# The first weight load split over two hardware DMA queues, in a one-core gated decode block

## The chip, the core and the metric

The kernel runs on 1 core of one Trainium2 chip. The metric is device time in microseconds, from the start to the end of one execution on that core. The kernel before took 376.38 us (median of 3 runs, 376.34 to 377.0).

A core has a matrix engine (TensorE, PE in the profile), VectorE (DVE), ScalarE (ACT), GpSimd (POOL) and SyncE (SP). Data comes from the device's memory by DMA: an engine's sequencer issues a transfer, and the transfer's packets are carried by the 16 DMA engines that the profile counts. A transfer belongs to the queue of the engine that issued it. The profile of before shows two queues of kind "hardware_dynamic": q1, on which everything that SP issues goes, and q10, on which ScalarE's one transfer goes.

## What is computed

One token for each of B = 2 sequences, width D = 448. With xn the layer norm of x, the output is x + s * g, where s is grouped-query attention of xn over a cache (16 query heads, 8 key/value heads, 4096 positions, head width 256) and g is the SiLU of a bilinear feed-forward of xn:

```
def _A_ref(x, k_cache, v_cache, wq, wo):
    q = (lambda x, *d: x.transpose(*d))((x @ wq).reshape(B, Sq, Hq, Dh), 0, 2, 1, 3)
    ...
    scores = jnp.einsum("bhqd,bhkd->bhqk", q, k) * (Dh ** -0.5)
    p = _softmax(scores, axis=-1)
    o = jnp.einsum("bhqk,bhkd->bhqd", p, v)
    return (lambda x, *d: x.transpose(*d))(o, 0, 2, 1, 3).reshape(B, Sq, Hq * Dh) @ wo

def _B_ref(x, w_gate, w_up, w_down):
    g = jnp.einsum("bsd,df->bsf", x, w_gate)
    u = jnp.einsum("bsd,df->bsf", x, w_up)
    h = g * u
    return jnp.einsum("bsf,fd->bsd", h, w_down)

x = A_x
xn = _layernorm(x, axis=-1)
s = _A_ref(xn, A_k_cache, A_v_cache, A_wq, A_wo)
g = _silu(_B_ref(xn, B_w_gate, B_w_up, B_w_down))
return x + s * g
```

All data are float32. Keys and values alone are 134 MB; with the weights the profile counts 158.5 MB read.

## The kernel before

The whole job is a stream of loads with a little work on each. There are 16 pairs of a key/value head and a sequence, i = 0 to 15. `ring` has two buffers of 64 KB per partition (8 MiB each): one takes `first` (the keys of pair 0), and then each takes a `vk` load, the values of pair i beside the keys of pair i + 1. `slot` is a single buffer that holds one weight at a time: first wq0 (the half of the query weights for the first heads), later w_gate with w_up (`wgu`), w_down with the other half of wq (`wdq`), and most of wo.

`plan` (line 82) writes the list of loads, and `issue(n)` (line 62) issues the next n of them from SP, in order. A load whose buffer is still in use waits at SP's queue, together with everything behind it. The list starts with wq0, `first`, and the first vk load; `issue(3)` at line 94 sends these three. wgu waits until TensorE has finished with wq0 (the end of `query(0)`), and the next vk load until the scores of pair 0 have been computed from `first`.

wq0 comes as one transfer of 128 partitions x 26,624 bytes (line 75). Its last rows are stored apart: `wqx` (line 79) brings 16 partitions x 16,384 bytes into columns of the same slot that lie behind wq0.

x itself is tiny (2 x 448). Line 102 loads it into `x2`, a view of the tile `e0` that `early()` makes at line 100, from ScalarE's queue. GpSimd makes the identity matrix `ident` at line 104. Then comes a chain on VectorE: mean, centred x, sum of squares (lines 114 to 118), the power on GpSimd (line 120), the normed rows (123, 124), four transposes on TensorE (127) that need `ident`, and the copy to `xnT` (129). A like branch gives `xeT` (139) for the rows in wqx. With these and wq0, `query(0)` (line 317) multiplies: in `rows`, 12 matmuls at line 173, then those of lines 179 and 182 with wqx. VectorE turns the result into `qT` (195), and `scores(0)` (line 321) starts on `first`.

In the main loop (line 324), step i multiplies the probabilities with the values of pair i (line 277), computes the scores of pair i + 1 (line 245), issues the next load, scales the output (331) and runs the softmax (246 to 270). Feed-forward, second query half and the projection are fitted in at steps 0, 2, 4 and 8. After the loop the last pairs, the projection from wo2's pieces (line 313), the gate and x are put together (380, 381) and written at line 382.

Of the kernel before, what the change touches and what calls it, by code (L numbers as in the profile page):

```python
# [29 lines left out]
SIDE = 16  # L30
EXTRA = 8
# [8 lines left out]
def gated_decode_block(ctx: ExitStack, tc: tile.TileContext, x, first, vk, last0, last1, wq0, wqx, wdq, wo, wgu, out):  # L40
    nc = tc.nc
# [17 lines left out]
    loaded = {}  # L59
    todo = []  # L60

    def issue(n=1):
        for names, src, cuts in todo[:n]:
            weight = names[0].startswith("w")
            if weight:
                t = slot.tile([128, PART], F32, name="slot", align_bytes=512)
            else:
                t = ring.tile([128, 2 * ROW], F32, name="ring", align_bytes=512)
            width = ROW if not weight else src.shape[1] // len(names)
            for i, name in enumerate(names):  # L70
                loaded[name] = t[:, i * width:(i + 1) * width]
            if names == ["wd", "wq1"]:
                loaded["wd"], loaded["wq1"] = t[:, :14 * D], t[:, 14 * D:]
            for lo, hi in zip(cuts, cuts[1:]):
                nc.sync.dma_start(t[:, lo:hi], src[:, lo:hi])  # L75
            if names == ["wq0"]:
                at = src.shape[1]
                loaded["wqx"] = t[:, at:at + EXTRA * 512]
                nc.sync.dma_start(loaded["wqx"][:SIDE], wqx[:, :4])
        del todo[:n]  # L80

    def plan(names, src, cuts=None):
        todo.append((names.split(), src, cuts or [0, src.shape[1]]))
# [7 lines left out]
            plan(*weights[i])  # L91
    plan(f"k{LAST + 1} v{LAST}", last0, [0, ROW, 2 * ROW])
    plan(f"v{LAST + 1} wo2", last1, [0, 4096, 7168, *(ROW + i * D // 2 for i in (0, 6, 12, 14, 15, 16))])
    issue(3)


    def early():
        return [work.tile([128, 2, 512], F32, name=n, bufs=1)[:B] for n in ("p", "pT")]

    e0, e1 = early()  # L100
    x2 = e0[:, 0, :D]
    nc.scalar.dma_start(x2, x)
    ident = const.tile([128, 128], F32)
    make_identity(nc, ident)
    one = const.tile([1, 1], F32)
# [30 lines left out]
    for j in range(NK):  # L136
        at = 384 + j * SIDE
# [65 lines left out]
    def lift(ps):  # L203
        t = work.tile([128, D], F32, name="h")
        nc.scalar.copy(t, ps[:, :D])
        return t
# [113 lines left out]
    oT2 = const.tile([128, 1, 2, REP, W], F32)  # L320
    ss = scores(0)
    issue(2)
    p = over(softmax(*ss))
    for i in range(LAST):
        g, b = divmod(i, B)
        o = bank("o", 1)
        values(i, p[0], o)
        ss = scores(i + 1)

        issue(1 + (i + 1 in weights))  # L330
        nc.scalar.activation(ob[:, b * 4 + g if g < 4 else b * 3 + g - 4], o, AF.Copy, scale=p[1])  # L331
        if i == LAST - 1:
            cb = combine(ob, 6)
        p = softmax(*ss)
        if i < LAST - 1:
            p = over(p)
        if i == 7:
            cb = combine(ob, 8)
            for n in range(B):
                turn(oT0, cb[:, n * 256:(n + 1) * 256], 0, n, 4)  # L340
            ob = work.tile([128, 8, 512], F32, name="ob", bufs=1)
        if i in (0, 2, 4, 8):
            if i == 0:
                ffn_in()
            if i == 2:
                ffn_out()
            if i == 4:
                query(1)
            if i == 8:
                project(oT0, 0, 0, EARLY)  # L350
# [6 lines left out]
    t = lift(wide)  # L357
# [76 lines left out]
```

## Time and profile before

| | before |
|---|---|
| runs | 376.34, 376.38, 377.0 us |
| the profiled execution's own time | 376.44 us |
| its span in the trace | 374.7 us |
| DMA packets | 4357, 158.79 MB |
| mean rate over the span | 424 GB/s |
| mean granted TensorE clock | 0.752 |

The span is shorter than the execution's time because the trace begins with the first instruction and ends with the last. The times in the lines below are microseconds from the start of the span. In a line of the timeline the columns are start, length, engine, line, operation, output<-input and count, and in brackets the engine's idle time before it and what ended that. "SPq" and "ACTq" are the sequencers that issue transfers. In a line of the windows stand the stretch, its length, the busy time of TensorE, its weight loads, VectorE, ScalarE and GpSimd, each with the number of instructions, then the granted clock, the DMA share (1.00 is all 16 engines busy) and GB/s. In a queue row stand packets, MB and the share of the time of 16 engines.

The page's list of issues gives, for the transfers of the start, their sizes and the time from issue to landing: wq0 3328.0 KB in 10.7 us, `first` 4096.0 KB in 21.4 us, wqx 256.0 KB and x 3.5 KB without a landing time.

### The profile page before, as it was taken

The numbers are of one execution on the slowest core, as the hardware profiler recorded it, in microseconds if no ns is written. First come the engines' busy times: TensorE is split into PE (matmuls) and PEld (weight loads), VectorE is DVE, ScalarE is ACT, GpSimd is POOL, SyncE is SP. The second block draws the span as 40 slices with busy tenths as digits, with TensorE's granted clock in tenths as the row PEclk, the third lists the DMA queues.
The fourth block names the chain that finished last, engine by engine and source line by source line (L and its number), as shares of the span: only waits on it lengthen the run. The fifth ranks groups of instructions, "written<-read, shape, count | busy, mean of one in ns | idle before, by whom it ended". The sixth has DMA issues, their size and how long they took to land.

```text
span 374.7 us, 3272 instructions
## 1 busy us (share of the span) xinstructions
PE 209.0 (56%) x1472; PEld 63.0 (17%) x1472; DVE 63.2 (17%) x113; ACT 36.3 (10%) x56; POOL 1.2 (0%) x7
## 2 busy tenths in 40 slices
PE   1792468174736092869174666641718191909795
PEld 0110112021211020212021112210202020202232
DVE  4003021103030003030303030300211203020431
ACT  1001010001012002010101010100010101010120
POOL 1000000000000000000000000000000000000000
PEclk9968586657686567789758687865968776877899
DMA  8999899999999999999999999999999999999994
GB/s 322 438 500 434 374 439 448 441 443 435 425 429 448 441 441 393 429 448 436 427 448 434 436 422 409 444 448 434 441 428 429 441 441 406 450 409 434 415 418 181
DMA packets 4357, 158.79 MB, mean 424 GB/s; under 512 B 614, under 2 KB 1000, under 8 KB 1384
## 3 DMA queue, kind: packets, MB, share of 16 engines
q1 hardware_dynamic: 4340, 158.59, 98.2%
q8 instruction: 11, 0.18, 0.2%
q10 hardware_dynamic: 4, 0.00, 0.0%
q14 instruction: 2, 0.02, 0.0%
HBM read 158.54 MB, written 0.06 MB: 423 GB/s over the span
## 4 chain that ended last, share of the span: by engine, by line
DMA 76%; PE 22%; issue 0%; SPq 0%; DVE 0%
DMA ring<-vk 67%; PE o L277 11%; PE s L245 8%; DMA ring<-last 6%; DMA slot<-wq 3%; PE t L179 1%; PE t L173 1%; PE t L182 1%; SPq L75 0%; PE acc L313 0%; DVE qT L195 0%; DVE h L380 0%; DVE h L381 0%
## 5 line engine op out<-in xcount | busy, mean ns | idle before, releaser
L277 PE MATMUL o<-ring,pT 128*32 128x512 f32 x480 | 83.1, 855 | 91.5 <-DMA ring<-vk 91.5
L245 PE MATMUL s<-ring,qT 128*32 128x512 f32 x512 | 61.8, 624 | 2.4 <-ACT p L260 1.5
L246 DVE TENSOR_REDUCE m<-s 128x1 f32<-128x1024 f32 x16 | 19.6, 1225 | 222.1 <-PE s L245 222.1
L277 PEld LDWEIGHTS o<-ring,pT 128*32 128x32 f32 x480 | 21.2, 149 | 143.6 <-issue 142.0
L331 ACT ACTIVATE ob<-o,su 128x512 f32<-128x512 f32 x14 | 9.6, 688 | 190.7 <-PE o L277 190.7
L260 ACT ACTIVATE p<-s,m 128x1024 f32<-128x1024 f32 x16 | 17.8, 1114 | 97.5 <-DVE m L257 97.5
L245 PEld LDWEIGHTS s<-ring,qT 128*32 128x32 f32 x512 | 18.0, 115 | 44.6 <-issue 40.4
L263 DVE STREAM_TRANSPOSE pT<-p 128x1024 f32<-128x1024 f32 x15 | 18.7, 1245 | 21.2 <-ACT p L260 21.2
L269 PE MATMUL sm<-su,add_head 128*128 128x1 f32 x32 | 7.6, 305 | 22.9 <-ACT p L260 22.9
L251 PE MATMUL sm<-ident,m 128*1 128x128 f32 x16 | 4.3, 270 | 18.9 <-DVE m L246 18.8
L253 DVE TENSOR_REDUCE mx<-sm 1x128 f32<-1x512 f32 x16 | 10.8, 678 | 6.3 <-PE sm L251 6.3
L173 PE MATMUL t<-slot,xnT 128*32 128x512 f32 x48 | 8.8, 887 | 3.4 <-DMA slot<-wq 3.4
L269 PEld LDWEIGHTS sm<-su,add_head 128*128 128x128 f32 x32 | 6.2, 242 | 25.4 <-ACT p L260 24.1
L256 PE MATMUL sm<-one,mx 1*128 1x1 f32 x16 | 3.5, 218 | 12.3 <-DVE mx L253 12.3
L304 PE MATMUL wide<-slot,oT 128*32 128x448 f32 x48 | 7.2, 759 | 0.0
L173 PE MATMUL s<-slot,xnT 128*32 128x448 f32 x48 | 7.2, 748 | 0.1
L227 PE MATMUL t<-slot,hT 128*32 128x448 f32 x28 | 5.6, 911 | 2.4 <-DMA slot<-wdq 2.4
L251 PEld LDWEIGHTS sm<-ident,m 128*1 128x1 f32 x16 | 1.3, 79 | 33.0 <-DVE m L246 32.3
L286 PE MATMUL cb<-ob,add_blocks 128*32 128x64 f32 (+2 forms) x64 | 5.6, 475 | 0.8 <-ACT ob L372 0.8
L179 PE MATMUL t<-slot,oT 16*32 16x512 f32 x16 | 5.7, 703 | 0.0
L195 DVE STREAM_TRANSPOSE qT<-t 128x256 f32<-128x256 f32 x4 | 1.6, 428 | 19.8 <-PE t L179 15.2
L256 PEld LDWEIGHTS sm<-one,mx 1*128 1x128 f32 x16 | 2.1, 133 | 15.4 <-DVE mx L253 15.4
(71 smaller groups left out, 54.1 us busy)
## 6 DMA issues: line engine op xcount, KB each, us to landing
ring<-last SPq DMA_DIRECT2D x2, 4096.0 KB, 24.8
slot<-wdq SPq DMA_DIRECT2D x1, 6720.0 KB
slot<-wgu SPq DMA_DIRECT2D x1, 6272.0 KB, 34.3
slot<-wo SPq DMA_DIRECT2D x1, 5376.0 KB, 40.9
ring<-first SPq DMA_DIRECT2D x1, 4096.0 KB, 21.4
slot<-wq SPq DMA_DIRECT2D x1, 3328.0 KB, 10.7
ring<-last SPq DMA_DIRECT2D x1, 2048.0 KB, 14.7
ring<-last SPq DMA_DIRECT2D x1, 1536.0 KB
```

What stands on the lines that cost most here:

```text
L173: nc.tensor.matmul(ps[W * c:W * (c + 1), :n], xnT[:, k, :], block(NT * k + c), start=k == 0, stop=False)
L179: nc.tensor.matmul(ps[W * c:W * (c + 1), :n], xeT[:, j, :], extra[:SIDE, at:at + n], start=False, stop=j == NK - 1)
L227: nc.tensor.matmul(ps[W * t:W * (t + 1), :D], hT[:, i], loaded["wd"][:, i * D:(i + 1) * D], start=i < NT, stop=i >= 14 - NT)
L245: nc.tensor.matmul(s[W * c:W * (c + 1), h, :], q[:, d], k[:, h, d, c, :], start=d == 0, stop=d == 1)
L246: nc.vector.tensor_reduce(m[:, 0:1], s, axis=AX.XY, op=OP.max)
L253: nc.vector.tensor_reduce(mx, sm[:1, None, :128].rearrange("p o (c j) -> p o j c", c=NT).to_broadcast([1, NT, W, NT]), axis=AX.X, op=OP.max)
L260: nc.scalar.activation(p, s, AF.Exp, bias=m[:, 1:2], scale=1.0 / 16, accum_out=su[:, 0:1])
L263: nc.vector.transpose(pT.rearrange("p h n -> p (h n)"), p.rearrange("p h n -> p (h n)"))
L269: nc.tensor.matmul(sm[:, 130:131], add_head.rearrange("p a r j -> p (a r j)"), su[:, 0:1], start=True, stop=True)
L277: nc.tensor.matmul(o[W * t:W * (t + 1), :], pT[:, h, at:at + 2 * W:2], loaded[f"v{i}"][:, e * 512:(e + 1) * 512], start=e < NT, stop=e >= ...
L304: nc.tensor.matmul(wide[W * t:W * (t + 1), :D], heads(oT, i, first), loaded["wo"][:, i * D:(i + 1) * D], start=i < NT, stop=i >= LATE - NT)
L331: nc.scalar.activation(ob[:, b * 4 + g if g < 4 else b * 3 + g - 4], o, AF.Copy, scale=p[1])
```

## The change

wq0 is issued in two halves: partitions 64 to 127 from ScalarE's queue and partitions 0 to 63 from SP's. Between them and wqx, x is loaded from GpSimd's queue. Since `x2` must exist by then, `issue(3)` is moved behind `early()`. On ScalarE the half of wq0 stands where x's load was, as its first instruction; on GpSimd x's load stands ahead of the three instructions that make `ident`; on SP the order stays wq0 (now half), wqx, `first`, vk and so on. All later loads are as before, line numbers move by three to nine, and the order of the work on TensorE and VectorE is the same.

```diff
@@ -71,12 +71,17 @@
             if names == ["wd", "wq1"]:
                 loaded["wd"], loaded["wq1"] = t[:, :14 * D], t[:, 14 * D:]
+            if names == ["wq0"]:
+
+                at = src.shape[1]
+                nc.scalar.dma_start(t[64:, :at], src[64:])
+                nc.sync.dma_start(t[:64, :at], src[:64])
+                nc.gpsimd.dma_start(x2, x)
+                loaded["wqx"] = t[:, at:at + EXTRA * 512]
+                nc.sync.dma_start(loaded["wqx"][:SIDE], wqx[:, :4])
+                continue
             for lo, hi in zip(cuts, cuts[1:]):
                 nc.sync.dma_start(t[:, lo:hi], src[:, lo:hi])
-            if names == ["wq0"]:
-                at = src.shape[1]
-                loaded["wqx"] = t[:, at:at + EXTRA * 512]
-                nc.sync.dma_start(loaded["wqx"][:SIDE], wqx[:, :4])
         del todo[:n]
@@ -91,15 +96,13 @@
     plan(f"v{LAST + 1} wo2", last1, [0, 4096, 7168, *(ROW + i * D // 2 for i in (0, 6, 12, 14, 15, 16))])
-    issue(3)
-
 
     def early():
         return [work.tile([128, 2, 512], F32, name=n, bufs=1)[:B] for n in ("p", "pT")]
 
     e0, e1 = early()
     x2 = e0[:, 0, :D]
-    nc.scalar.dma_start(x2, x)
+    issue(3)
     ident = const.tile([128, 128], F32)
     make_identity(nc, ident)
```

## The prediction

> **What bounds the kernel now.** I began with the page: the engines' shares, the DMA row of the forty slices and the queue rows.
>
> ```profile
> span 374.7 us, 3272 instructions
> PE 209.0 (56%) x1472; PEld 63.0 (17%) x1472; DVE 63.2 (17%) x113; ACT 36.3 (10%) x56; POOL 1.2 (0%) x7
> DMA  8999899999999999999999999999999999999994
> ...
> q1 hardware_dynamic: 4340, 158.59, 98.2%
> q8 instruction: 11, 0.18, 0.2%
> q10 hardware_dynamic: 4, 0.00, 0.0%
> ```
>
> No compute engine is busy for more than 56% of the span, while the packets of one queue, q1, fill 98.2% of the time of all 16 DMA engines. q10 carries four packets of almost no bytes: that is x, the only load that ScalarE issues. Next I asked whether the DMA engines ever run dry in between, with the windows (the last two columns are the DMA share and GB/s).
>
> ```profile
> 50.00:100.00 50.00, 27.52 (x184) 7.99 (x180) 7.99 (x12) 3.84 (x7) 0.00 (x0) 0.69 1.01 435
> ...
> 200.00:250.00 50.00, 29.19 (x188) 9.19 (x188) 10.74 (x17) 4.99 (x8) 0.00 (x0) 0.76 1.00 433
> ...
> 300.00:340.00 40.00, 21.84 (x148) 6.73 (x144) 6.72 (x10) 3.79 (x6) 0.00 (x0) 0.71 0.99 426
> ```
>
> They don't: 426 to 435 GB/s with a share of about 1 from 50 to 340 us. The chain of waits, in order of time, begins and goes on like this:
>
> ```profile
> 0.74 10.72 DMA slot<-wq
> ...
> 24.16 5.73 PE s L245 x32
> 29.89 0.02 issue
> 29.91 47.01 DMA ring<-vk
> 76.92 0.14 issue
> 77.06 6.53 PE o L277 x32
> 83.59 3.47 PE s L245 x32
> 87.06 0.02 issue
> 87.08 44.35 DMA ring<-vk
> ```
>
> It names some 10 us of TensorE between two loads. Read beside the windows this isn't time lost: while TensorE works on one ring buffer (77.06 to 87.06), the load of the other is running at 435 GB/s. The real bound is one stream of bytes: 158.59 MB at 433 GB/s are 366.3 us of the 374.7. What delays or advances the whole stream at its start comes out at the end one for one, and what delays only the compute early on costs nothing.
>
> So the start of the stream matters:
>
> ```profile
> 0.00:1.50 1.50, 0.00 (x0) 0.00 (x0) 0.09 (x2) 0.19 (x1) 0.70 (x6) 1.00 0.00 0
> 1.50:1.75 0.25, 0.00 (x0) 0.00 (x0) 0.00 (x0) 0.25 (x1) 0.00 (x0) 1.00 0.13 7
> 1.75:2.00 0.25, 0.00 (x0) 0.00 (x0) 0.00 (x0) 0.25 (x1) 0.00 (x0) 1.00 4.09 958
> 2.00:4.00 2.00, 0.00 (x0) 0.00 (x0) 1.29 (x4) 0.59 (x1) 0.00 (x0) 1.00 0.74 280
> 4.00:6.00 2.00, 0.14 (x2) 0.14 (x2) 1.27 (x5) 0.00 (x0) 0.55 (x1) 1.00 0.99 426
> ```
>
> A packet is booked where it starts, which is why one window shows 958; 2 to 4 us then shows only 280, and from 4 us on it is 426. The first rows of wq0 thus start at about 1.75 us, 1.0 us after the issue at 0.74, and come in unevenly.
>
> **The change part by part.** The issues and the chain of x, from the timeline:
>
> ```profile
> 0.74 0.53 ACTq L102 DMA_DIRECT2D p<-x  x1
> 0.74 0.39 SPq L75 DMA_DIRECT2D slot<-wq  x1
> 1.02 0.29 POOL masks.py:199 TENSOR_SCALAR_AFFINE_SELECT ident<-ident 128x128 f32<-128x128 f32 x1
> 1.18 0.79 SPq L79 DMA_DIRECT2D slot<-wqx  x1
> 2.02 0.41 SPq L75 DMA_DIRECT2D ring<-first  x1
> 2.61 0.61 DVE L114 TENSOR_REDUCE st<-p 2x1 f32<-2x448 f32 x1 [1.72 <-DMA p<-x]
> 5.86 0.58 PE L127 MATMUL t<-ident,pT 2*128 2x2 f32 x4 [5.86 <-DVE pT L123]
> 6.48 0.29 DVE L129 COPY xnT<-t 128x128 f32<-128x128 f32 x1 [0.52 <-PE t L127]
> 11.60 4.28 PE L173 MATMUL t<-slot,xnT 128*32 128x512 f32 x24 [3.42 <-DMA slot<-wq]
> 23.32 0.33 SPq L75 DMA_DIRECT2D slot<-wgu  x1
> 42.93 2.79 PE L277 MATMUL o<-ring,pT 128*32 128x512 f32 x12 [8.60 <-DMA ring<-vk]
> ```
>
> *x through GpSimd.* In this trace GpSimd issues no DMA, so the price has only bounds. On ScalarE, x was there 1.87 us after its issue (0.74 to 2.61); it can hardly be faster elsewhere, and slower is likely. Behind it stands a chain of 4.16 us up to the end of xnT (2.61 to 6.77). wq0 is ready at 11.6, so x may land 4.8 us later, at 7.4, before TensorE notices. If even that cover were gone, query(0) would slip, and behind it SP's wait to issue wgu, at 23.32 now. But at that moment `first` and the first vk load, 12 MiB, are still running, and the vk load lands only at 42.9; the stream would run dry only if the slip were near 18 us. GpSimd's issue stands ahead of the identity matrix, whose last instruction ends at 1.31 and is needed at 5.86: 4.5 us of cover. I take 0 for x and for the identity, with 0 as both ends: neither stands in the stream, so an earlier x gains nothing either (what its two packets take from the engines is counted below).
>
> *Issue order.* SP's issue covers 64 rows rather than 128; wqx, `first` and vk move up behind it by at most its 0.39 us, while the engines have rows of wq0 until about 11 us: 0. ScalarE loses x's issue and gains another in the same place; its next instructions are a table load and a copy at 8.23: 0. SP's wait for wgu now covers one landing more, long past by 23 us: 0.
>
> *What two queues can gain.* Both halves are issued at 0.74 by two sequencers. wq0 has 3328 KB, 3.41 MB, 8.0 us at 426 GB/s; landing took 10.72. Of the 2.72 us above that, 1.0 lies ahead of the first row, on either queue. The other 1.7 (late engines, slow first rows, the last receipt) bounds the gain; 0 is the other end. Only the part that is due to one queue having to name 128 rows in turn is open to the edit, and the issue of 0.39 us, halved, is the nearest row. I take 0.3: a little more than that 0.2, for late engines.
>
> [...]
>
> *What two queues can cost.* Now every DMA engine has two lists of rows to serve. 128 rows over 16 engines are 8 rows each, 4 from each list, of 26.6 KB or 0.99 us (q1: 98.2% of 16 x 374.7 us for 158.59 MB, 37.1 us per MB). Served in turn, that is 7 changes of list. The nearest row for a change is q8: its 11 lone packets, between rows of q1, took 0.2% of 5995 us; with the rounding, 9.0 to 15.0 us, 0.82 to 1.36 us for each 16.4 KB. At q1's rate it would be 0.61, so the excess is 0.21 to 0.75 us. [...] I take 0.4, inside the measured excess but below its middle, because those were packets that came alone to their queue. 7 x 0.4 = 2.8 us, bounds 0 and 5.3. Nothing covers it, as the stream has no idle time to give.
>
> Sum against the profiled execution (span 374.7, with 1.74 around it 376.44, which is 0.06 above the median of the runs): 376.44 - 0.3 + 2.8 + 0 = 378.94. I forecast **378.9 us**, slower by 0.7%.
>
> **The rivals.**
>
> *Halves.* All 16 engines could write the same 64 partitions at the same time, turn about. If one half of the partitions takes only half of the rate, wq0 takes 16.0 us instead of 8.0, up to +8.0 us. It decides from the point where the engines stand within one row (0.99 us) of each other in their turns, and the start is that close (0.13 of an engine before 1.75, 4.09 in the next quarter). But a lag within the row lets part of them write the other half; a lag of 0.3 us would spare 0.3/0.99, or 30%, and leave 5.6, hence 376.4 + 5.6 = 382.0. For it: one issue time for both halves. Against it: this trace has no 64-partition load that would show half a rate. [...]
>
> *A clean start.* Faster: two lists per engine are fetched side by side, late engines start with the rest, and x's small packets no longer stand ahead of wq0 on the hardware queues. That takes between half and all of the 1.7 us: about 1.0 off, 375.4. For it: the 280 GB/s between 2 and 4 us. Against it: part of the 1.7 is the receipt, which stays, and the end needs all 16 engines to gain.
>
> *Nothing to see.* Rows of both lists are fetched ahead and the changes cost nothing, and only the 0.3 is left: 376.1. That is also the case where the edit doesn't do what it says, because both queues feed the same 16 engines, which were already full.
>
> **How the numbers follow.** The measurement of this kernel can tell about 0.2%, 0.75 us, from no change. Changes of list (378.9; its own range 377.3 to 381.5): 0.36. Halves (382.0): 0.22. Clean start (375.4): 0.30. Nothing to see (376.1): 0.12. So slower 0.58, within 0.2% 0.12, faster 0.30. The range is 375.3 to 383.2: it leaves out about 0.05 of the clean start's best part (beyond 1.1 us), and about 0.06 of the halves near their full 8.0.
>
> **What would show it.** The forecast holds if the row of q10 carries about 1.7 MB, if both halves of wq0 land 2 to 3 us later than 11.46 us, with fewer GB/s than 426 between 4 and 10 us, and if the middle windows stay at 426 to 435, so that the lag at the first vk landing (42.9 now) is found again at the end. For halves the rate between 4 and 12 us would be near 213 to 280. For the clean start the 2 to 4 us window would rise well above 280 and wq0 would land before 10.8. x is rightly priced if TensorE's first matmul of query(0) still waits for wq0 and not for xnT. I am wrong if the middle windows change, or if the time moves without the landing of the first loads moving.

## The result, and the profile after

| | before | changed |
|---|---|---|
| median of the runs | 376.37 us (6 runs, 376.33 to 377.0) | 384.48 us (6 runs, 384.35 to 384.7) |
| ratio | | 1.0211, 95% interval 1.02 to 1.0222 |
| the profiled execution's span | 374.7 us | 382.7 us |

The changed kernel is slower by 8.1 us, 2.1%. Of all executions in this document one, of the first experiment (390.9 us), was in a slower state of the chip and is left out of that experiment's time and ratio.

The queue rows of its page come first (packets, MB, share of the time of 16 engines):

```profile
q1 hardware_dynamic: 4276, 156.89, 96.1%
q10 hardware_dynamic: 80, 1.70, 2.1%
q8 instruction: 11, 0.18, 0.2%
q0 software_dynamic: 32, 0.00, 0.0%
```

The change does what it says: half of wq0, 1.70 MB, goes on q10, and x on a queue of its own, q0. But 1.70 MB take 2.1% of the engines' time (16 x 382.7 us), where 158.59 MB took 98.2% of theirs before: about 75 us of an engine per MB instead of 37. On average a row of that half took twice as long. The windows (the last columns are DMA share and GB/s) show the same for the time of both halves:

```profile
4.00:6.00 2.00, 0.00 (x0) 0.00 (x0) 0.00 (x0) 0.00 (x0) 0.00 (x0) 1.00 0.98 200
6.00:8.00 2.00, 0.00 (x0) 0.00 (x0) 0.00 (x0) 0.00 (x0) 0.00 (x0) 1.00 0.84 174
8.00:10.00 2.00, 0.00 (x0) 0.00 (x0) 0.00 (x0) 0.00 (x0) 0.00 (x0) 1.00 1.19 267
10.00:12.00 2.00, 0.00 (x0) 0.00 (x0) 0.00 (x0) 0.00 (x0) 0.00 (x0) 1.00 1.00 226
...
20.00:24.00 4.00, 4.00 (x20) 0.90 (x17) 0.00 (x0) 0.00 (x0) 0.00 (x0) 1.00 1.01 434
```

```profile
4.00:18.00 14.00, 0.83 (x8) 0.65 (x8) 2.85 (x9) 0.00 (x0) 0.56 (x1) 1.00 1.00 217
```

Single windows of 2 us swing between 174 and 267 GB/s, because a packet is booked where it starts; the long window gives the mean. From 4 to 18 us the DMA share is 1.00: the engines are not short of work. Yet the rate is 217 GB/s, about half of 426; once wq0 is in it is 434, as before. That the share stays full while the rate halves is what to see here: a busy share alone doesn't tell that a transfer is slow.

The queue rows of shorter stretches show in which order the engines took the two lists. A row of wq0 is one packet of 26.6 KB:

| stretch, us | queue | packets | MB | share of 16 engines |
|---|---|---|---|---|
| 2.0 to 7.5 | q10 | 48 | 1.28 | 109.1% |
| 7.5 to 9.5 | q1 | 16 | 0.43 | 94.3% |
| 9.5 to 11.5 | q10 | 16 | 0.43 | 94.0% |
| 11.5 to 17.5 | q1 | 48 | 1.28 | 100.6% |

(The few packets of x and other packets of almost no bytes, at most 1.7% of a stretch, are left out.) So the 16 engines work on one list at a time, and but for the edges of the stretches all of them write the same 64 partitions. The records don't name the engine of a packet, but 16 packets that fill about 94% of 16 engines' time are one row for each engine: three rows from q10, one from q1, one from q10, three from q1. That is 3 changes of list for an engine, not the 7 of the forecast.

The list of issues (KB, time from issue to landing) and the timeline show where the delay goes:

```profile
slot<-wq ACTq DMA_DIRECT2D x1, 1664.0 KB, 14.7
slot<-wq SPq DMA_DIRECT2D x1, 1664.0 KB, 18.9
...
p<-x POOLq DMA_DIRECT2D x1, 3.5 KB, 12.2
```

```profile
0.74 0.55 ACTq L77 DMA_DIRECT2D slot<-wq  x1
0.74 0.57 SPq L78 DMA_DIRECT2D slot<-wq  x1
1.25 0.69 POOL L79 DMA_DIRECT2D p<-x  x1 [0.80 <-POOLq L428]
...
13.50 0.61 DVE L117 TENSOR_REDUCE st<-p 2x1 f32<-2x448 f32 x1 [12.61 <-DMA p<-x]
...
17.39 0.29 DVE L132 COPY xnT<-t 128x128 f32<-128x128 f32 x1 [0.52 <-PE t L130]
...
19.81 4.97 PE L176 MATMUL t<-slot,xnT 128*32 128x512 f32 x24 [0.72 <-DMA slot<-wq]
...
34.81 0.33 SPq L84 DMA_DIRECT2D slot<-wgu  x1
...
50.64 5.78 PE L280 MATMUL o<-ring,pT 128*32 128x512 f32 x32 [3.85 <-DMA ring<-vk]
```

wq0 is complete at 19.6 us instead of 11.5, the first vk load is used at 50.64 instead of 42.93, 7.7 us later, and the end of the chain of waits is shifted by about as much, 8.0 us: the last pieces land at 378.03 instead of 370.06.

```profile
356.05 21.98 DMA ring<-last
378.03 0.14 issue
378.16 1.45 PE acc L316 x48
```

In between the stream is as full as before, 431 to 437 GB/s from 50 to 300 us:

```profile
50.00:100.00 50.00, 28.40 (x200) 8.28 (x200) 7.99 (x12) 4.32 (x7) 0.00 (x0) 0.81 1.00 431
...
250.00:300.00 50.00, 23.81 (x166) 7.05 (x158) 5.82 (x10) 3.47 (x5) 0.00 (x0) 0.70 1.01 437
```

So 8 us were lost in the first 20 us, and nothing gave them back.

### The profile page after: what moved, and what is told of

It reads as the page before. It is cut to its first block, busy times and chain, and to the rows that moved or that the text cites. A ratio compares the mean times of both kernels' runs of the same rounds, so it can differ in the third digit from the quotient of the medians.

```text
span 382.7 us, 3274 instructions
## 1 busy us (share of the span) xinstructions
PE 210.4 (55%) x1472; PEld 62.4 (16%) x1472; DVE 63.2 (17%) x113; ACT 36.2 (9%) x56; POOL 2.0 (1%) x8
## 4 chain that ended last, share of the span: by engine, by line
DMA 76%; PE 21%; SPq 1%; DVE 1%; issue 0%; ACT 0%; ACTq 0%
DMA ring<-vk 70%; PE o L280 12%; PE s L248 7%; DMA ring<-last 6%; PE t L176 1%; SPq L84 1%; PE acc L316 0%; DVE m L249 0%; ACT p L263 0%; PE t L189 0%; SPq L81 0%; DVE mx L256 0%; PE sm L272 0%; SPq L78 0%; DVE h L383 0%
## 5 line engine op out<-in xcount | busy, mean ns | idle before, releaser
L280 PE MATMUL o<-ring,pT 128*32 128x512 f32 x480 | 81.4, 840 | 89.5 <-DMA ring<-vk 89.5
L249 DVE TENSOR_REDUCE m<-s 128x1 f32<-128x1024 f32 x16 | 19.6, 1224 | 218.0 <-PE s L248 218.0
L254 PE MATMUL sm<-ident,m 128*1 128x128 f32 x16 | 4.3, 270 | 18.9 <-DVE m L249 18.8
L259 PE MATMUL sm<-one,mx 1*128 1x1 f32 x16 | 3.7, 228 | 12.4 <-DVE mx L256 12.4
L176 PE MATMUL t<-slot,xnT 128*32 128x512 f32 x48 | 9.9, 994 | 0.7 <-DMA slot<-wq 0.7
L182 PE MATMUL t<-slot,oT 16*32 16x512 f32 x16 | 7.4, 942 | 0.0
## 6 DMA issues: line engine op xcount, KB each, us to landing
slot<-wq ACTq DMA_DIRECT2D x1, 1664.0 KB, 14.7
slot<-wq SPq DMA_DIRECT2D x1, 1664.0 KB, 18.9
```

The lines of the kernel that those rows point to most:

```text
L176: nc.tensor.matmul(ps[W * c:W * (c + 1), :n], xnT[:, k, :], block(NT * k + c), start=k == 0, stop=False)
L182: nc.tensor.matmul(ps[W * c:W * (c + 1), :n], xeT[:, j, :], extra[:SIDE, at:at + n], start=False, stop=j == NK - 1)
L249: nc.vector.tensor_reduce(m[:, 0:1], s, axis=AX.XY, op=OP.max)
L280: nc.tensor.matmul(o[W * t:W * (t + 1), :], pT[:, h, at:at + 2 * W:2], loaded[f"v{i}"][:, e * 512:(e + 1) * 512], start=e < NT, stop=e >= ...
```

## The experiments

Two theories stood first. H: in the changed kernel the 16 engines write into the same half of the partitions at a time (the table above shows that they do), and a half takes only half of the rate. L: an engine pays for each change between two lists of rows, as the forecast had it. All edits are to the code of the first load; "before" stands for the kernel before, run beside each on the same chip (376.46 us, in one group 376.47).

**Both halves on one queue** (the kernel before, edited):

```diff
-                nc.sync.dma_start(t[:, lo:hi], src[:, lo:hi])
+                for r in parts:
+                    end = r + 64 if len(parts) > 1 else 128
+                    nc.sync.dma_start(t[r:end, lo:hi], src[r:end, lo:hi])
```

with `parts = range(0, 128, 64)` for wq0 and `[0]` for all other loads.

> The kernel before, with wq0 as two transfers of 64 partitions, both on SP's queue; x stays on ScalarE's. Theory H (all engines write into the same half of the partitions at a time, and a half takes only half of the rate): 384 to 385 us, as the changed kernel, with wq0 complete near 19 us and about 213 GB/s until then. Theory L (an engine pays for each change between two lists of rows): there is one list and no change, so 376.4.

Measured: 385.39 us, ratio 1.0239 (1.0223 to 1.0254). The windows of this run:

```profile
4.00:18.00 14.00, 1.42 (x16) 0.87 (x16) 2.01 (x13) 0.25 (x1) 0.55 (x1) 1.00 0.97 201
```

One queue, no change of list, and the loss is there, so L isn't needed to explain it. Theory H expected a little less, 384 to 385 us and 213 GB/s; what makes up the difference is not shown.

**Four transfers of 32 partitions on one queue** (64 replaced by 32 in that edit). Here and in what was expected of later runs, a "way into the destination" is my name for whatever limits the rate at which a set of partitions is written; no run shows what it is or how many there are.

> The kernel before, with wq0 as four transfers of 32 partitions on SP's queue. Theory H, if 32 partitions next to each other reach as many ways into the destination as 64 do: 384 to 385 us again. If the rate goes with the number of partitions instead: a quarter of the rate, 32 us for wq0 instead of 8, about 400 us. Theory L: 376.4.

Measured: 385.18 us (1.0213 to 1.0244). A transfer of 32 partitions isn't slower than one of 64 (from 4 to 16 us 202 GB/s here, 200 in the run before this one); between these two the rate doesn't go with the number of partitions. (The run in eighths, below, shows that it does fall with 16, to 123 GB/s.)

**Two queues, divided by columns** (the changed kernel, edited):

```diff
-                nc.scalar.dma_start(t[64:, :at], src[64:])
-                nc.sync.dma_start(t[:64, :at], src[:64])
+                nc.scalar.dma_start(t[:, at // 2:at], src[:, at // 2:])
+                nc.sync.dma_start(t[:, :at // 2], src[:, :at // 2])
```

> The changed kernel, but each queue brings half of the columns of wq0 to all 128 partitions; x on GpSimd's queue as in the changed kernel. Theory H: the loss is gone, 375.8 to 376.8 us. Theory L: each engine has 8 rows of 13.3 KB from each list; at the 8.1 us lost by 7 changes, 1.2 us each, up to 15 changes cost 17 us, 393; at least as much as the changed kernel, 384.

Measured: 376.67 us, ratio 1.0002 (0.9994 to 1.0011). The windows and the timeline:

```profile
4.00:10.00 6.00, 0.00 (x0) 0.00 (x0) 1.73 (x4) 0.00 (x0) 0.00 (x0) 1.00 1.02 433
```

```profile
8.16 0.61 DVE L117 TENSOR_REDUCE st<-p 2x1 f32<-2x448 f32 x1 [7.27 <-DMA p<-x]
12.06 0.29 DVE L132 COPY xnT<-t 128x128 f32<-128x128 f32 x1 [0.52 <-PE t L130]
...
14.11 2.79 PE L176 MATMUL t<-slot,xnT 128*32 128x512 f32 x12 [0.36 <-ACT xg L152]
```

Two lists per engine, with twice as many rows, run at 433 GB/s: the changes between the two lists, both full, cost nothing that can be seen (0.2 us of 376.46, with 1 inside the interval of the ratio), and L falls. And there is a second finding. Here x is late (VectorE starts on it at 8.16, before at 2.61), wq0 no longer hides that, and TensorE starts query(0) at 14.11 instead of 11.60. The time doesn't notice: the compute at the start has the second cover that was claimed for it, the loads already on their way.

**x alone on GpSimd's queue** (wq0 in one transfer on SP's queue, x as in the changed kernel).

> The kernel before with x on GpSimd's queue and wq0 in one transfer on SP's. Theory H: x is not what costs, 376.0 to 376.7 us. If x on GpSimd's queue were the cause, through its late landing: 384. x itself should land within about 6 us of its issue, since rows take 1 us instead of 2.

Measured: 376.48 us, ratio 1.0001 (0.9993 to 1.001). x lands 6.5 us after its issue instead of 12.2, a little more than expected, and costs nothing.

So it is the partitions. The next runs ask which partitions, all but one of them on SP's queue alone with x as before.

**The middle half and two outer quarters**, `parts = [slice(32, 96), slice(0, 32), slice(96, 128)]`. The slow transfers so far wrote 32 or 64 neighbouring partitions on one side of partition 64. For the 64 from 32 to 95, which lie across it, nothing was measured yet: H takes the full rate for them as an assumption, and for the two quarters at the edges half of it, as the run in quarters had it (202 GB/s).

> The kernel before, with wq0 on SP's queue as partitions 32 to 95, then 0 to 31, then 96 to 127. [...] wq0 takes 4 + 4 + 4 = 12 us instead of 8: 380.4 us. Theory N (any transfer of 64 partitions or fewer is slow because of its number of rows): 384.5, as with the halves 0 to 63 and 64 to 127.

Measured: 381.52 us, +5.05, ratio 1.0129 (1.0112 to 1.0146). The windows:

```profile
4.00:6.00 2.00, 0.58 (x4) 0.50 (x4) 0.79 (x5) 0.00 (x0) 0.55 (x1) 1.00 0.99 426
8.00:14.00 6.00, 0.00 (x0) 0.00 (x0) 0.00 (x0) 0.01 (x1) 0.00 (x0) 1.00 1.00 213
```

Within one load, 64 partitions across the middle run at 426 GB/s, and the 32 at each edge run at 213. That excludes N and agrees with H. The expected loss of 4.0 us was about 1.1 short.

**The same with other source rows.** The middle could have been fast because of what is read:

```diff
+            parts = [(slice(32, 96), slice(0, 64)), (slice(0, 32), slice(64, 96)), (slice(96, 128), slice(96, 128))]
...
+                    nc.sync.dma_start(t[r, lo:hi], src[f, lo:hi])
```

> As the run with partitions 32 to 95, 0 to 31 and 96 to 127, but filled from the rows 0 to 63, 64 to 95 and 96 to 127 of wq0 in device memory, so the first half of the rows comes from the addresses of the slow case and goes to the partitions of the fast one (the weights stand in other partitions than the matmuls expect). Theory H/R (the destination decides): first 1664 KB at 426 GB/s, 381.0 to 382.0 us. Theory S (the read side, rows 0 to 63 of the source, is slow): first 1664 KB at 213 GB/s, 384.5 us or more.

Measured: 381.23 us (1.0108 to 1.0139). The run is for its time alone, as its output isn't the block's.

```profile
4.00:6.00 2.00, 0.58 (x4) 0.49 (x4) 0.79 (x6) 0.00 (x0) 0.55 (x1) 1.00 0.95 399
8.00:14.00 6.00, 0.00 (x0) 0.00 (x0) 0.00 (x0) 0.00 (x0) 0.00 (x0) 1.00 1.00 213
```

The first 1664 KB land 8.2 us after the issue (7.9 in the run before this one; the first of the two halves on one queue took 11.3). The rows that were slow are fast when they go to partitions 32 to 95. The writing side decides.

**Even, then odd partitions**, `parts = [slice(0, 128, 2), slice(1, 128, 2)]`. Theory R takes 64 partitions that are spread over all 128 to run like all 128, an assumption before this run.

> The kernel before, with wq0 on SP's queue as the 64 even partitions and then the 64 odd ones. [...] Theory R (what counts is how many ways the whole transfer reaches): 376.4 us. [...]

Measured: 376.89 us, ratio 1.001 (1.0001 to 1.002).

```profile
4.00:10.00 6.00, 1.42 (x16) 0.87 (x16) 2.00 (x13) 0.25 (x1) 0.55 (x1) 1.00 0.99 426
```

R holds, with a remainder of 0.4 us: a transfer of 64 partitions, every second one, runs at 426 GB/s, as all 128 did. Which engine writes which row within it, no run here shows.

**Even and odd on two queues** (the changed kernel with `t[1::2, :at]` from `src[1::2]` on ScalarE's queue and `t[0::2, :at]` from `src[0::2]` on SP's).

> The changed kernel, two queues and x on GpSimd's, but ScalarE's queue brings the odd partitions and SP's the even ones. Theory R: each transfer reaches every way into the destination, so the loss is gone: 376.2 to 377.0 us, with x late as in the run by columns. If two queues for two sets of partitions cost by themselves: up to 384.5.

Measured: 376.72 us, ratio 1.0004 (0.9995 to 1.0013).

```profile
4.00:10.00 6.00, 0.00 (x0) 0.00 (x0) 0.81 (x3) 0.00 (x0) 0.00 (x0) 1.00 1.02 440
```

In the changed kernel nothing was altered but which 64 partitions go on which queue, and the whole loss of 8 us is gone. The packet records of this trace come in the same turns as in the changed kernel, 48 rows of q10, 16 of q1, 16 of q10 and 48 of q1, so the 3 changes of list are all still there; the half on q10 lands 8.9 us after its issue and that on q1 10.8, as in the changed kernel q10's came first (14.7 and 18.9). This run doesn't beat the kernel before either, nor do the columns: no run here shows a gain from a second queue.

**Eighths**, eight transfers of 16 partitions on SP's queue.

> The kernel before, with wq0 as eight transfers of 16 partitions on SP's queue. [...] If a smaller transfer is never slower than half: 384.5.

Measured: 396.85 us (2 runs), +20.4, ratio 1.0538 (1.0517 to 1.0559).

```profile
4.00:28.00 24.00, 1.42 (x16) 0.87 (x16) 2.02 (x13) 0.25 (x1) 0.55 (x1) 1.00 1.04 123
```

The rate is 123 GB/s, 0.29 of 426, where 32 partitions ran at 202. So a smaller transfer can be much slower than half; the answer of 384.5 was 12.4 us short.

**One vk load in halves, in mid-kernel** (`parts = [slice(0, 64), slice(64, 128)]` where the load is `v5`).

> The kernel before, with one vk load in the middle (the values of pair 5 and the keys of pair 6, 8.39 MB) as two transfers of 64 partitions on SP's queue; wq0 as before. At half of 426 to 433 GB/s it takes 39 us instead of 19.5. Theory H and a stream without slack: +19.5, 395.9 us. If the compute of the loop had slack to hide a late load in mid-kernel: less, down to 376.4.

Measured: 404.16 us, +27.7, ratio 1.0729 (1.0712 to 1.0746): more than either answer.

```profile
100.00:140.00 40.00, 21.38 (x148) 6.16 (x143) 3.63 (x6) 4.66 (x7) 0.00 (x0) 0.71 1.00 432
140.00:160.00 20.00, 5.77 (x36) 1.96 (x32) 3.36 (x5) 2.49 (x3) 0.00 (x0) 0.58 1.12 289
160.00:180.00 20.00, 11.74 (x88) 3.01 (x80) 4.14 (x7) 1.89 (x3) 0.00 (x0) 0.84 1.00 207
180.00:200.00 20.00, 1.03 (x8) 0.43 (x12) 0.00 (x0) 0.00 (x0) 0.00 (x0) 0.50 0.91 206
200.00:240.00 40.00, 22.50 (x152) 6.73 (x147) 6.72 (x10) 3.79 (x6) 0.00 (x0) 0.71 1.00 431
```

From 140 to 200 us 20 x (289 + 207 + 206) GB/s, 14.0 MB, were moved. At 433 GB/s it would have been 26.0 MB. The missing 12 MB are 27.6 us, the whole loss: in mid-kernel too the stream has no slack, and each microsecond comes out at the end. But a load of 8.39 MB at half rate would have missed 8.39 MB, not 12. At the 206 to 207 GB/s of the windows it takes 40.6 us instead of 19.4, which is 21 us of the 27.7. The packet records show the rest: 9.9 MB in rows of 64 KB, not 8.39, took over 1.5 times their usual 2.4 us, so rows of the neighbouring loads were slow as well, and some rows at the two ends of the slow stretch took nearly three times as long. Why is open; how the engines stand to one another in mid-kernel no run shows.

## Why the prediction was wrong

The forecast had the direction right by luck: the term that made it slower measured nothing, and the loss came from the rival to which I had given 0.22. The signs written down beforehand told the two apart. The halves of wq0 landed 4.0 and 8.2 us after 11.46, not 2 to 3, and the 217 GB/s from 4 to 18 us lie in the band that was named for the halves, 213 to 280.

**What bounds the kernel: right.** One stream of bytes without slack; the 8 us lost in the first 20 stand at the end, and a loss in mid-kernel does so too.

**x, the identity, the order of issues at nothing: right.** x landed 12.2 us after its issue, at about 13.5, later than the 7.4 that I had named as the point where TensorE would notice. It noticed nothing only because wq0 itself was late (19.81 <- wq0). The 7.4 was too late a point anyway. I had ended the chain of x at xnT, but the first matmul of query(0) also waits until ScalarE has copied `xg` out of the one buffer of the tile `t` that both use; the run by columns shows this wait (14.11 <- ACT xg). Before, that copy ended at 8.48, 3.1 us ahead of the matmul at 11.60, so the cover was 3.1 us rather than 4.8. The identity, two instructions of GpSimd, was ready at 2.52 in the changed kernel and needed at 16.77. In the run by columns the first cover was gone, TensorE started 2.5 us later, and the second cover held. Even wgu's issue, 11.5 us later in the changed kernel (34.81 against 23.32), added nothing.

**The gain of 0.3 us: not shown.** With the loss taken away (columns, even and odd on two queues) the ratios are 1.0002 and 1.0004, with 1 inside both intervals. The row behind the 0.3, SP's issue of 0.39 us for 128 rows, didn't halve with the rows: for 64 it took 0.57 in the changed kernel. Of the 1.7 us that bounded the gain, 0.3 lie between the end of wq0's last row, 11.17 in the packet records of before, and its landing at 11.46.

**The step that failed: 7 changes of list at 0.4 us, 2.8 us.** There were 3 changes, not 7: the engines did not take the lists in strict turn. And the runs put the price of a change at no more than their uncertainty. With even and odd partitions on two queues, the same 3 changes gave 376.72 us against 376.46, with 1 inside the interval of the ratio; with columns, up to 15 changes gave 376.67. The row of q8 was the wrong neighbour: it was of packets that come alone to their queue, and a full list beside a full list is another case. What the excess in q8's row consists of isn't shown. I had 0 as the lower bound, an estimate of mine, and then took 0.4; no run shows a price of that size.

**The rival that held: halves.** In place of a price for changes, the runs show a price for the partitions written. The mechanism was right, all engines on the same 64 partitions at a time, and its full price too: 16.0 us instead of 8.0 for wq0, 376.4 + 8.0 = 384.4, against 384.48 measured. The half rate was an assumption when I wrote it; for the halves 0 to 63 and 64 to 127 the runs show 201 to 217 GB/s. I reduced it to 5.6 us for a lag of 0.3 us between engines, a lag that no row showed, and cut the range at 383.2. The measured 217 GB/s, against 213 for half of 426, leave no clear sign that a lag spared anything. "This trace has no 64-partition load" was counted as evidence against; it was only a lack of evidence.

## What to carry to other kernels

A transfer to SBUF should spread over the partitions as those did that ran at the full rate here, 426 to 440 GB/s: all 128, some columns of all 128, every second one, or the middle 64. Partitions 0 to 63 or 64 to 127 alone moved at about half the rate, 201 GB/s on one queue and 217 on two, and the DMA share still read 0.97 and 1.00, so look at GB/s. In this kernel the DMA engines are full nearly from start to end (98.2% of their time on q1 alone, before), and a second queue gave nothing (ratios 1.0002 and 1.0004). A bound for a price that no row shows must be carried in full into the range.

## What the runs showed of the hardware that was not expected

- A load of 64 partitions ran at 201 to 217 GB/s or at 426, depending on which partitions it wrote: 0 to 63 and 64 to 127 slow, 32 to 95 fast, even or odd ones fast.
- Two full queues were not served in strict turn in the changed kernel: in rounds of 16 packets came three of one queue, one of the other, one of the first and three of the other.
- Transfers of 16 partitions ran at 123 GB/s, 0.29 of 426, where those of 32 ran at 202.
- In a full stream, x on GpSimd's queue took 6.5 to 7.8 us to land when wq0 ran at full rate (x alone, columns, even and odd on two queues), and 12.2 us beside the slow halves; from ScalarE's queue, issued at 0.74 ahead of the stream's first rows, it was ready 1.9 us after its issue.
- A slow load in mid-kernel cost 27.7 us where its own bytes at half rate account for 19.5.
